# A recurrent attention layer and an FFN on one core: from 128-step chunks with per-head products to 64-step chunks with block-diagonal 128x128 products and the FFN woven in

## The chip, the cores and the metric

The kernel runs on one core of one Trainium2 chip. The time is that of the core from its first to its last instruction, in device microseconds (us). Each comparison is made on one chip, with runs of the kernel before among the others. The engines are PE (TensorE, with PEld for its weight loads), DVE (VectorE), ACT (ScalarE), POOL (GpSimd) and SP (SyncE), which only issues DMAs here.

## The reference, cut to what matters

```python
# 4 batches x 8 heads, 768 steps, head_dim 40; per head a 40x40 state
for t in range(S):
    y[:, :, t] = einsum('bhd,bhde->bhe', rt, state)
    Sa    = einsum('bhde,bhe->bhd', state, at)
    state = state * wt[:, :, None, :] - einsum('bhd,bhe->bhde', Sa, bt) \
            + einsum('bhd,bhe->bhde', vt, kt)
x = y.transpose(0, 2, 1, 3).reshape(3072, 320)       # tokens x (heads*40)
out = square(maximum(x @ w_in, 0)) @ w_out           # 320 -> 2048 -> 320
```

A kernel does not walk 768 steps. It takes a chunk of steps at once: products of k, b, a, r and v of the chunk, scaled by cumulative products of w, give the outputs within the chunk under a causal mask, and a 40x40 state per head is carried from chunk to chunk.

## The kernel before

Six chunks of 128 steps. Each chunk is prepared (cumulative decays by FP32 products, transposes of r, v, k, a), then worked in eight quads of four heads. A head has 40 channels, so an operand indexed by channel occupies 40 rows of the array, and one indexed by time 128. After the last chunk the FFN runs alone.

```python
# prep, once per chunk (FP32 products)
nc.tensor.matmul(out=cs[:, 0:n], lhsT=UTI[:], rhs=lnW[:, s0:s1], ...)      # FP32
nc.tensor.matmul(out=rep[:, 0:8*D], lhsT=SEL127[:], rhs=GAM[:, c0:c0+8*D], ...)
# stage2, once per quad: 40-row and 128-row weights alternate
for i in range(4):
    nc.tensor.matmul(out=mstp[:, i, :], lhsT=AT[pb:pb + D, prs[i], :],      # 40 rows
                     rhs=ST2[pb:pb + D, prs[i], :], start=True, stop=False)
    nc.tensor.matmul(out=mstp[:, i, :], lhsT=Em[:, i, :],                   # 128 rows
                     rhs=Vp[:, hhs[i], 0:D], start=False, stop=True)
...
for i in range(4):
    nc.tensor.matmul(out=xtp[:, i, :], lhsT=AT[pb:pb + D, prs[i], :],       # 40 rows
                     rhs=Zb[pb:pb + D, i, :], start=True, stop=False)
    nc.tensor.matmul(out=xtp[:, i, :], lhsT=Em[:, i, :],                    # 128 rows
                     rhs=CmT[:, i, :], start=False, stop=True)
... # yp, ytmp, YS, stp, state, and 32 small DMAs per chunk that gather YS into XT
# then the FFN, 512 tokens at a time
for g in range(3):
    nc.tensor.matmul(out=hp[:], lhsT=WIN[g][:, j*128:(j+1)*128],
                     rhs=XTg[g][:, tb*512:(tb+1)*512], start=(g==0), stop=(g==2))
nc.scalar.activation(out=hsb[:], in_=hp[:], func=ACTF.Copy)
nc.vector.scalar_tensor_tensor(out=Gt[:, j, :], in0=hsb[:], scalar=0.0, in1=hsb[:],
                               op0=ALU.max, op1=ALU.mult)
```

The scheduler of the framework decides the order of instructions on each engine, within the data dependences; the source order is a hint to it.

## Time and profile before

The median is 550.71 us (2 runs, 549.3 to 552.12).

| stretch | us | what stands out |
|---|---|---|
| start | about 45 | input DMA, first prep |
| six chunks | about 387 | PE busy 97%, clock 0.66 |
| FFN | about 118 | PE busy 97%, clock 0.98 |

The page, parts 1 and 2: the busy time of each engine, and tenths of 40 equal slices of the span.

```profile
PE 500.9 (91%) x3570; PEld 304.5 (55%) x3576; DVE 292.6 (53%) x478; ACT 230.4 (42%) x403; POOL 49.3 (9%) x54
...
PE   0609999999999999999999999999999799999997
...
PEclk9957566856559558595668755796555799999999
```

PE looks full from the start to the end, but the PEclk row (the granted clock) shows that through the chunks it was mostly granted half to two thirds of its clock, and steadily all of it only in the FFN (last eight slices). The view by windows says the same in numbers. Its columns are the window, its length, busy time and count for each engine, granted clock, DMA share and GB/s.

```profile
130.00:190.00 60.00, 58.10 (x465) 36.92 (x464) 35.65 (x62) 22.46 (x39) 4.65 (x5) 0.66 0.33 53
...
435.00:550.00 115.00, 111.39 (x652) 64.24 (x655) 59.92 (x92) 65.32 (x116) 0.00 (x0) 0.99 0.10 35
```

The timeline inside a quad. Columns: start, duration, engine, line, operation, output<-inputs, rows*columns of the weights, the moving tile, count.

```profile
153.33 0.31 PE L292 MATMUL yp_1357<-XmT,Btn 128*40 128x128 bf16 x1
...
153.44 0.31 PE L290 MATMUL yp_1357<-CmT,Kp 128*40 128x128 bf16 x1
...
154.03 0.28 PE L282 MATMUL xtp_1585<-Zb,AT 40*128 40x128 bf16 x1
...
154.25 0.29 PE L284 MATMUL xtp_1585<-CmT,Em 128*128 128x128 bf16 x1
...
154.47 0.29 PE L282 MATMUL xtp_1585<-Zb,AT 40*128 40x128 bf16 x1
```

Read the starts, not the durations, because matmuls are pipelined. The yp products, all with 128-row weights, start 0.105 us apart (the mean of six starts; the two shown differ by 0.11). The xtp products, whose weights alternate between 40 and 128 rows, start 0.22 us apart. Both move 128 columns, at the same clock (0.50 in that window).

### The profile page before, as it was taken

The page shows a single profiled execution, that of the slowest core. Times are in us where ns is not written, and L with a number is a line of the kernel's source. Part 1 is how long each engine was busy: PE and PEld are TensorE (multiplying, and loading weights), DVE is VectorE, ACT ScalarE, POOL GpSimd, SP SyncE. Part 2 cuts the span into 40 slices and gives each one's busy share as a digit, 9 for nine tenths or more (in the row PEclk, how much of TensorE's full clock was granted, in tenths as well). Part 3 has the DMA queues.
Part 4 walks back from the last instruction along what each step waited for, and adds up shares of the span by engine and source line. Part 5 has one row for each costly group of instructions (what it writes and reads, how often), then busy time and mean ns, then how long its engine had stood idle before and what let it go on. Part 6 is the DMA issues. An engine that isn't in the chain of part 4 may idle for free.

```text
span 550.1 us, 8764 instructions
## 1 busy us (share of the span) xinstructions
PE 500.9 (91%) x3570; PEld 304.5 (55%) x3576; DVE 292.6 (53%) x478; ACT 230.4 (42%) x403; POOL 49.3 (9%) x54
## 2 busy tenths in 40 slices
PE   0609999999999999999999999999999799999997
PEld 0207546655667545765557665576666365566554
DVE  0126448634566446755467553775655536634752
ACT  1705542644125532255324325352112446744762
POOL 9903000011000200002001010000000000000000
PEclk9957566856559558595668755796555799999999
DMA  9999335633327330934108291000000010011011
GB/s 159 189 186 180 53 54 80 76 53 51 53 49 109 54 51 8 146 56 82 27 7 117 39 128 26 6 6 8 7 7 10 4 49 17 33 48 37 19 42 50
DMA packets 163577, 32.69 MB, mean 59 GB/s; under 512 B 158096, under 2 KB 163216, under 8 KB 163536
## 3 DMA queue, kind: packets, MB, share of 16 engines
q1 hardware_dynamic: 161088, 29.50, 34.5%
q0 software_dynamic: 2448, 2.62, 2.8%
q8 instruction: 28, 0.46, 0.4%
q14 instruction: 13, 0.11, 0.1%
HBM read 28.84 MB, written 3.93 MB: 60 GB/s over the span
## 4 chain that ended last, share of the span: by engine, by line
PE 86%; DMA 5%; SPq 3%; ACT 2%; DVE 2%; issue 1%; ACTq 0%; DVEq 0%
PE hp L360 11%; PE trp L198 5%; PE cs L157 5%; PE rep L181 4%; DMA NB<-in_b_dram 4%; SPq L131 3%; PE trw L213 2%; ACT Zb L271 1%; ACT AT L204 1%; DVE Ap L175 1%; PE op_5950 L374 0%; PE op_5910 L374 0%; PE op_5717 L374 0%; PE op_5544 L374 0%; PE op_5371 L374 0%
## 5 line engine op out<-in xcount | busy, mean ns | idle before, releaser
L367 DVE SCALAR_TENSOR_TENSOR Gt<-hsb 128x512 bf16<-128x512 bf16 x96 | 62.5, 692 | 49.6 <-ACT hsb L366 49.6
L366 ACT ACTIVATE hsb<-hp 128x512 bf16<-128x512 f32 x96 | 57.1, 597 | 12.3 <-DMA XT_82<-YS 5.5
L157 PE MATMUL cs<-lnW,UTI 128*128 128x512 f32 (+1 forms) x36 | 30.9, 972 | 18.7 <-ACT lnW L148 18.7
L374 PEld LDWEIGHTS <-Gt 128*128 128x128 bf16 x384 | 37.6, 98 | 15.5
L181 PE MATMUL rep<-GAM,SEL_74 128*128 128x320 f32 x48 | 25.8, 666 | 14.6 <-DVE GL_166 L187 14.2
L360 PE MATMUL hp<-XT_80,WIN_93 128*128 128x512 bf16 x96 | 37.5, 391 | 0.5 <-issue 0.2
L360 PE MATMUL hp<-XT_78,WIN_90 128*128 128x512 bf16 x90 | 35.0, 389 | 3.0 <-ACT hsb L366 2.4
L360 PE MATMUL hp<-XT_82,WIN_96 128*128 128x512 bf16 x96 | 37.6, 392 | 0.0
L297 DVE TENSOR_TENSOR YS<-ytmp,GT 40x512 bf16<-40x512 f32 x48 | 32.7, 681 | 0.5
L274 PEld LDWEIGHTS <-AT 40*128 40x128 bf16 x192 | 19.0, 99 | 20.1 <-issue 13.1
L292 PEld LDWEIGHTS <-Btn 128*40 128x40 bf16 x192 | 24.0, 130 | 11.0 <-issue 9.2
L284 PEld LDWEIGHTS <-Em 128*128 128x128 bf16 x192 | 19.3, 101 | 19.4 <-issue 2.1
L282 PEld LDWEIGHTS <-AT 40*128 40x128 bf16 x192 | 18.7, 98 | 19.1 <-issue 4.7
L290 PEld LDWEIGHTS <-Kp 128*40 128x40 bf16 x192 | 23.6, 123 | 4.1 <-issue 2.2
L276 PEld LDWEIGHTS <-Em 128*128 128x128 bf16 x192 | 19.5, 101 | 10.1 <-issue 2.8
L145 ACT ACTIVATE Rp<-NR 128x1280 bf16<-128x1280 f32 x6 | 7.6, 1269 | 40.7 <-PE trp L198 30.6
L181 PEld LDWEIGHTS rep<-GAM,SEL_74 128*128 128x128 f32 x48 | 11.5, 273 | 19.6 <-issue 17.0
L172 DVE TENSOR_TENSOR Kp<-NK,GAMI 128x1280 bf16<-128x1280 f32 x6 | 8.9, 1488 | 24.3 <-ACT GAMI L160 24.3
L157 PEld LDWEIGHTS cs<-lnW,UTI 128*128 128x128 f32 x36 | 9.1, 306 | 22.8 <-issue 20.8
L143 POOL MEMSET Rp<- 128x768 bf16 x6 | 4.5, 745 | 179.4 <-PE trp L198 179.4
L304 PEld LDWEIGHTS <-Vp 128*40 128x40 bf16 x192 | 15.1, 110 | 9.4 <-issue 7.3
L267 PEld LDWEIGHTS <-S_84 40*40 40x40 bf16 x192 | 14.9, 115 | 9.4 <-issue 6.0
(1138 smaller groups left out, 1074.1 us busy)
## 6 DMA issues: line engine op xcount, KB each, us to landing
NR<-in_r_dram SPq DMA_DIRECT2D x6, 640.0 KB
NK<-in_k_dram SPq DMA_DIRECT2D x6, 640.0 KB
NV<-in_v_dram SPq DMA_DIRECT2D x6, 640.0 KB
NW<-in_w_dram SPq DMA_DIRECT2D x6, 640.0 KB
NA<-in_a_dram SPq DMA_DIRECT2D x6, 640.0 KB
NB<-in_b_dram SPq DMA_DIRECT2D x6, 640.0 KB
out_dram<-osb SPq DMA_DIRECT2D x24, 160.0 KB
WOUT<-in_moe_w_out_dram POOLq DMA_DIRECT2D x1, 1280.0 KB, 14.5
```

The lines of the kernel that those rows point to most:

```text
L157: nc.tensor.matmul(out=cs[:, 0:n], lhsT=UTI[:], rhs=lnW[:, s0:s1], start=True, stop=True)
L181: nc.tensor.matmul(out=rep[:, 0:8 * D], lhsT=SEL127[:], rhs=GAM[:, c0:c0 + 8 * D], start=True, stop=True)
L198: nc.tensor.transpose(out=trp[:, j * L:(j + 1) * L], in_=srcv, identity=IDb[:])
L276: nc.tensor.matmul(out=mstp[:, i, :], lhsT=Em[:, i, :], rhs=Vp[:, hhs[i], 0:D], start=False, stop=True)
L284: nc.tensor.matmul(out=xtp[:, i, :], lhsT=Em[:, i, :], rhs=CmT[:, i, :], start=False, stop=True)
L290: nc.tensor.matmul(out=yp[pb:pb + D, i, :], lhsT=Kp[:, hhs[i], 0:D], rhs=CmT[:, i, :], start=(i == 0), stop=False)
L292: nc.tensor.matmul(out=yp[pb:pb + D, i, :], lhsT=Btn[:, hhs[i], 0:D], rhs=XmT[:, i, :], start=False, stop=(i == 3))
L297: nc.vector.tensor_tensor(out=YS[pb:pb + D, pc:pc + 4, :], in0=ytmp[pb:pb + D, :, :], in1=GT[pb:pb + D, pc:pc + 4, 0:L], op=ALU.mult,)
L360: nc.tensor.matmul(out=hp[:], lhsT=WIN[g][:, j * 128:(j + 1) * 128], rhs=XTg[g][:, tb * 512:(tb + 1) * 512], start=(g == 0), stop=(g == 2),)
L366: nc.scalar.activation(out=hsb[:], in_=hp[:], func=ACTF.Copy)
L367: nc.vector.scalar_tensor_tensor(out=Gt[:, j, :], in0=hsb[:], scalar=0.0, in1=hsb[:], op0=ALU.max, op1=ALU.mult,)
L374: nc.tensor.matmul(out=op_[:], lhsT=Gt[:, j, s_ * 128:(s_ + 1) * 128], rhs=WOUT[:, j, :], start=(j == 0), stop=(j == 15),)
```

## The change

The intent: the array is always used as one 128x128 square, PE's waits are filled with FFN products, and PE's idle time shrinks. Two heads from different batches are paired. k and b of one chunk of 64 steps are stacked along the partitions, and so are a and r; a and r are then transposed into block-diagonal form (ARB), so that one 128x128 product serves both heads. A second step corrects the solve of the triangular system. The FFN of chunk c-1 (input products) and c-2 (output products) is emitted inside the units of chunk c. There are 12 chunks of 4 units of 4 pairs, that is 48 units. The FP32 products of the preparation become two bf16 products each, of a high and a low part (lhi, llo).

The names in the diff and in the traces: ef is the product of kt (k and b, transposed) with the a half of ARB, and em is ef under the causal mask; mp, mb, mc are the steps of the solve; tv and vt are its transposed result; cx is vt's product with r, and cm is cx under the mask; sp is the state, yp the output of attention; hp, hs, g and op belong to the FFN; GI and GP are the cumulative decays, and gr, GLI, GLT the decay row that ends the chunk. The diff, cut to its core (the old body is removed whole):

```diff
-    L = 128
+    L = 64
+    NU = 4
+    def load_rv(c):                       # r and v: POOL's DMA queue, cast to bf16 on the way
+            nc.gpsimd.dma_start(out=AR[c % 2][64:128, :, s, 0:D], in_=r[...])
+            nc.gpsimd.dma_start(out=VM[c % 2][p0:p0 + 64, :, s, 0:D], in_=v[...])
+    # zero fills AR, VM, KB, STB, SB on DVE; ARB on POOL; then masks UTI, UTE, MSK on POOL
...
+    def prep_k(c):
+            nc.vector.tensor_tensor(out=kb[o, :, s, 0:D], in0=n["K"][q], in1=gi[q], op=ALU.mult)
+        gr = drp.tile([2, NPAIR, D], FP32, ...)                  # DRAM
+        nc.sync.dma_start(out=gr[:], in_=gi[63:128:64])          # the decay row
+                nc.sync.dma_start(out=gli[64*s:64*s+D, :], in_=gr[s].rearrange("x e -> e x"))
+        nc.vector.reciprocal(out=glt[:], in_=gli[:])
...
+    def prep_tr(c, u):
+        nc.scalar.activation(out=kt[:], in_=tk[:], func=ACTF.Copy)
+        nc.vector.tensor_copy(out=arb[0:64, 4*u:4*u+4, 0:4:2, :], in_=ta[0:64]...)
+        nc.vector.tensor_copy(out=arb[64:128, 4*u:4*u+4, 1:4:2, :], in_=ta[64:128]...)
+    def st_ef(c, u):  ... em = ef * MSK                          # DVE
+    def st_m0(c, u):  ... mb = -mp, two halves                   # ACT
+    def st_cor(c, u): ... vm = mb - mc, two halves               # DVE
+    def st_tvm(c, u): ... vt = copy(tv)                          # DVE
+    def st_cx(c, u):
+        nc.scalar.activation(out=cm[:], in_=cx[:]..., func=ACTF.Copy)
+        for s in range(2):
+            nc.gpsimd.affine_select(out=cm[q], in_=cm[q], pattern=[[0, 8], [1, 64]], ...)
+    def st_st(c, u):  ... STB = sp * GLT, two halves             # DVE
+    def st_y(c, u):   ... ys = yp * gp, two halves               # DVE
+    def st_ts(c, u):  ... SB = copy(tp), two halves              # DVE
+    def ff_in(c, jj):
+        nc.scalar.activation(out=hs[:], in_=hp[:], func=ACTF.Relu)
+        nc.vector.tensor_tensor(out=G[c][:, 2*jj:2*jj+2, :], in0=hs[:], in1=hs[:], op=ALU.mult)
...
+    prep_head(0)
+    for u in range(3):
+        prep_tr(0, u)
+    N[1] = load(1)
+    load_rv(1)
+    load_weights()
...
+    for n, (c, u) in enumerate(units):
+        st_tvm(c, u); ff_in(c - 1, 2*u); st_cx(c, u); st_ef(*nx); ff_out(c - 2, 2*u)
+        ... prep of chunk c+1 ...; st_m0(*nx); ff_in(c - 1, 2*u + 1); st_st(c, u)
+        st_y(c, u); st_cor(*nx); ff_out(c - 2, 2*u + 1); st_ts(c, u); prep_tr(*units[n + 3])
```

## The prediction

> **What bounds it now.** The profile page gives PE 500.9 us busy of 550.1 (91%), DVE 292.6, ACT 230.4. Windows of the trace split the span: about 45 us until the first chunk is prepared (the chain of waits there is input DMA), six chunks of 57 to 65 us in which PE is busy 97% but at a granted clock of only 0.66 to 0.71, and an FFN of 118 us at 0.98 that streams without gaps. So attention is 387 us, held by PE's instruction stream, not by arithmetic. In the timeline, at clock 0.50, products that alternate 40-row and 128-row weights (xtp) take 220 ns each, unmixed ones of the same width (yp) 105 ns; unmixed 128x128 transposes at clock 1.00 take 56 ns. The Trainium skill (TensorEngine Tiling, Key Properties) says that changing tiling mode drains TensorE; the mixed products agree.
>
> **The change.** Full 128x128 weights everywhere, FP32 products as bf16 high plus low, FFN woven in. From the instruction order: 48 units (12 chunks x 4), each about 72 products and 11,800 streamed columns: 4.9 us at clock 1.00, about 6.2 at 0.8. PE's work thus falls to about 240 to 300 us, and FFN products fill its waits.
>
> **What it adds is DVE work.** Per unit, with durations of before (512 columns from PSUM fp32 673 ns; 160 columns 317 ns; bf16 PSUM copy of 1024 692 ns, so 512 about 0.42 us; fp32 product of 1280 1488 ns, so 640 about 0.82): em 0.67, vt 0.42, correction 0.64, state 0.64, y 0.64, block-diagonal copies 0.84, state transpose 0.48, squares 2 x 0.42, xt 0.18, prep 6.4/4 = 1.6. Sum 6.9 us, 333 us in all (estimate), perhaps 15 less where neighbours overlap. The 0.42 of the squares assumes that two bf16 SBUF operands run at double rate, as the skill says (VectorE: DVE Perf Modes, perf-mode tier table); no instruction of before shows it. The half-partition pairs (64 x 160) pay the roughly 150 ns fixed part twice. ACT about 4.4 us per unit (211 us, with 11 pairs of table loads of 1.28), POOL about 3 (two selects of about 0.63, memsets, DMA issue).
>
> **Sum.** DVE becomes the busiest engine. Start about 20 us (half-size chunk, w first), tail about 10 us of FFN output products. Between, DVE's 320 us at 85 to 90% use: the unit's chain mc-vm-tv-vt-cx and ef-em-mp-mb-mc crosses PE, DVE and ACT, PE executes in order, three PSUM buffers serve ten tiles per unit, and the scheduler bunches FFN input products into one half of each chunk and output products into the other. That gives about 370 us. Total 400 us, range 355 to 445. Chances: faster 0.96, same 0.02, slower 0.02.
>
> **What would show it right.** DVE busy 310 to 340 us; a steady pitch of 7 to 8.5 us per unit, 28 to 34 per chunk; clock 0.75 to 0.95; 128-column products at 56 to 107 ns; squares near 420 ns; first unit at about 20 us; tail of at most 15 us.
>
> **What would make it wrong.** DVE squares or copies at single rate (plus 25 us or more); PE stalled for DVE, ACT or PSUM buffers so that the clock stays near 0.6 and PE becomes the limit again (430 or more); POOL's DMA issue and selects late for cx or v; slow small DMAs (the decay row through DRAM, scattered bf16 r and v) holding a chunk; or DVE instructions overlapping more than before (350 or less).

## The result, and the profile after

The changed kernel takes 448.28 us (2 runs, 446.34 to 450.22), and the ratio to the kernel before is 0.8131, with a 95% interval of 0.8028 to 0.8235. Repeated on another chip (run a0 below) it is 448.39 us and 0.8167 (0.8120 to 0.8215). A ratio here is the mean time of one kernel's runs over that of the other's runs of the same rounds, so it is not quite the ratio of the medians quoted. The direction was right, but 448 lies above the forecast's 400 and just outside its range of 355 to 445: the gain was 102 us where 151 was forecast.

The page after, parts 1, 2 and 4 (the last is the chain of waits, followed back from the end):

```profile
PE 315.3 (71%) x3480; PEld 221.3 (50%) x3480; DVE 350.7 (79%) x820; ACT 205.0 (46%) x394; POOL 149.7 (34%) x257
...
PE   0231767877877877877876886876877778777975
...
DVE  7442787997997997996997997997987987977841
...
PEclk9999998989999999998999989999999998999989
...
issue 41%; POOL 25%; PE 17%; DVE 16%; POOLq 0%; ACT 0%; DVEq 0%
```

PE's busy time fell by 186 us and its clock is now nearly full. DVE is the busiest engine. Two things stand out: in slices 2 to 4 (about 11 to 44 us) little runs: 4, 4 and 2 tenths on DVE, 2, 3 and 1 on PE, and the last two slices are thin. The windows view of the changed kernel, with the same columns as before:

```profile
20.00:40.00 20.00, 3.57 (x29) 2.81 (x28) 7.35 (x14) 2.23 (x5) 0.00 (x0) 1.00 1.12 171
...
140.00:180.00 40.00, 30.54 (x362) 21.75 (x363) 34.65 (x83) 22.07 (x42) 14.31 (x25) 1.00 0.54 55
...
420.00:445.00 25.00, 16.72 (x138) 11.43 (x135) 7.68 (x23) 6.68 (x12) 2.00 (x6) 0.90 0.11 28
```

From 20 to 40 us PE is busy for 3.57 of 20 us, DVE for 7.35 and POOL not at all, while the DMA engines move 171 GB/s. In the middle DVE is busy 34.65 of 40 us.

In the timeline, the 48 copies of vt mark the units. The first starts at 44.5 us, the last at 422.2, and between them the distance repeats every four units (8.06, 10.7, 7.2, 6.6 us), 32.6 us per chunk. The span of 444.3 us of the profiled run is therefore 44.5 + 377.7 + 22.1. The forecast had 20 + 370 + 10. **The middle was nearly right. The start and the tail were not.** The cut is not quite the forecast's: the first vt copy comes 4 us after em, DVE's first instruction of unit 0 proper, so this middle holds 47 of the 48 units. Counted by whole units, the middle is 386 us (48 x 8.04), and start and tail together are 59 us, where the forecast had 30.

The start in the timeline of the changed kernel (brackets: idle time of the engine before the instruction, and what ended it):

```profile
14.73 8.83 SPq L59 DMA_DIRECT2D NK<-in_k_dram  x2
...
17.75 0.45 PE L157 MATMUL cs<-lhi,UTI 128*128 128x320 bf16 x1 [17.75 <-POOL UTI L112]
...
18.44 1.21 POOL L132 DMA_DIRECT2D WOUT<-in_moe_w_out_dram  x1
...
23.60 4.22 SPq L59 DMA_DIRECT2D NB<-in_b_dram  x1
...
27.94 4.19 SPq L169 DMA_DIRECT2D gr<-GI  x1
...
36.48 0.85 SPq L172 DMA_DIRECT2D GLI<-gr  x2
...
39.21 0.25 DVE L174 RECIPROCAL GLT<-GLI 128x16 f32<-128x16 f32 x1 [12.12 <-DMA GLI<-gr]
...
40.39 0.69 DVE L223 TENSOR_TENSOR em<-ef,MSK 128x512 bf16<-128x512 f32 x1
```

First, PE's first product waits 17.75 us for the mask UTI, because the scheduler placed the masks on POOL behind zero fills and eleven DMA issues. Second, the decay row (gr, then GLI) was ready to leave at 19.5 us, when GI was done, but SP was still issuing chunk 1's loads, and issues that take 0.8 us each elsewhere take 4 us here. Third, the reciprocal of the decay row stands in front of em in DVE's list of instructions, so DVE, and with it everything, waits 12.12 us for two transfers of 2.5 KB. (In run e4 below the reciprocal stands later, and em runs at 25.0 us, before it.)

The tail, in PE's and ACT's lines of the timeline:

```profile
427.44 7.18 PE L339 MATMUL hp<-xt,WIN 128*128 128x256 bf16 x48 [0.45 <-DVE xt L329]
...
434.46 2.34 PE L352 MATMUL op<-WOUT,g 128*128 128x320 bf16 x16
...
437.32 2.33 PE L352 MATMUL op<-WOUT,g 128*128 128x320 bf16 x16 [0.53 <-ACT osb L357]
...
439.69 0.44 ACT L357 ACTIVATE osb<-op 128x320 f32<-128x320 f32 x1 [2.42 <-PE op L352]
```

After the last vt copy, 5.2 us finish the unit, 7.0 us are the last chunk's FFN input products, 5.2 us its output products, and 4.6 us pass from osb to the end, with the last store. The forecast had counted the output products alone.

### The profile page after: what moved, and what is told of

Same layout as the page of the kernel before. It is cut to its first block, busy times and chain, and to the rows that moved or that the text cites. A ratio compares the mean times of both kernels' runs of the same rounds, so it can differ in the third digit from the quotient of the medians.

```text
span 444.3 us, 9156 instructions
## 1 busy us (share of the span) xinstructions
PE 315.3 (71%) x3480; PEld 221.3 (50%) x3480; DVE 350.7 (79%) x820; ACT 205.0 (46%) x394; POOL 149.7 (34%) x257
## 4 chain that ended last, share of the span: by engine, by line
issue 41%; POOL 25%; PE 17%; DVE 16%; POOLq 0%; ACT 0%; DVEq 0%
POOL cm L270 15%; PE hp L339 6%; POOL AR L68 4%; DVE VM L249 3%; DVE em L223 2%; PE op L352 2%; DVE ys L306 2%; PE yp L297 2%; DVE ARB L204 2%; POOL ARB L82 2%; DVE ARB L201 2%; DVE SB L315 1%; POOL VM L289 1%; POOL VM L288 1%; PE cx L265 1%
## 5 line engine op out<-in xcount | busy, mean ns | idle before, releaser
L270 POOL TENSOR_SCALAR_AFFINE_SELECT cm<-cm 64x512 bf16<-64x512 bf16 x96 | 77.2, 804 | 243.0 <-ACT cm L267 198.1
L343 ACT ACTIVATE hs<-hp 128x512 bf16<-128x512 f32 x96 | 57.2, 596 | 73.7 <-DVE g L344 39.9
L339 PE MATMUL hp<-xt,WIN 128*128 128x256 bf16 x576 | 87.0, 277 | 1.4 <-DVE xt L329 1.3
L352 PE MATMUL op<-WOUT,g 128*128 128x320 bf16 x384 | 70.6, 305 | 5.6 <-DVE g L344 4.7
L339 PEld LDWEIGHTS <-WIN 128*128 128x128 bf16 x576 | 54.6, 100 | 11.2 <-issue 2.4
L223 DVE TENSOR_TENSOR em<-ef,MSK 128x512 bf16<-128x512 f32 x48 | 32.6, 678 | 22.9 <-PE ef L221 22.6
L196 ACT ACTIVATE kt<-tk 128x512 bf16<-128x512 bf16 x48 | 28.6, 596 | 45.7 <-PE tk L194 45.7
L237 ACT ACTIVATE VMB<-mp 64x160 bf16<-64x160 f32 x96 | 28.6, 298 | 36.1 <-PE mp L233 34.8
L344 DVE TENSOR_TENSOR g<-hs 128x512 bf16<-128x512 bf16 x96 | 39.2, 426 | 6.8 <-ACT hs L343 5.4
L352 PEld LDWEIGHTS <-g 128*128 128x128 bf16 x384 | 33.0, 99 | 20.1 <-DVE g L344 11.5
L297 PE MATMUL yp<-KB,cm 128*128 128x80 bf16 x192 | 21.3, 209 | 28.9 <-POOL cm L270 28.8
L285 DVE TENSOR_TENSOR STB<-sp,GLT 64x160 bf16<-64x160 f32 x96 | 30.7, 320 | 13.4 <-PE sp L282 12.5
L306 DVE TENSOR_TENSOR ys<-yp,GP 64x160 bf16<-64x160 f32 x96 | 30.9, 322 | 4.9 <-PE yp L297 3.2
L194 PE MATMUL tk<-IDb,KB 128*128 128x128 bf16 x192 | 20.7, 236 | 10.3 <-DVE ys L306 6.8
L68 POOL DMA_DIRECT2D AR<-in_r_dram x24 | 19.7, 827 | 22.6 <-PE hp L339 20.1
```

Source lines behind the costliest of these rows:

```text
L68: nc.gpsimd.dma_start(out=AR[c % 2][64:128, :, s, 0:D], in_=r[2 * s:2 * s + 2, :, sl, :].rearrange("b h t e -> t (b h) e"))
L223: nc.vector.tensor_tensor(out=em[:], in0=ef[:], in1=MSK[:].rearrange("p (x y) t -> p x (y t)", y=2), op=ALU.mult)
L270: nc.gpsimd.affine_select(out=cm[q], in_=cm[q], pattern=[[0, 8], [1, 64]], compare_op=ALU.is_gt, fill=0.0, base=0, channel_multiplier=-1)
L285: nc.vector.tensor_tensor(out=STB[q, us, s, 0:D], in0=sp[q, :, s, :], in1=GLT[c % 2][q, us].unsqueeze(2).broadcast_to((64, 4, D)), op=ALU. ...
L297: nc.tensor.matmul(out=yp[:, i], lhsT=cm[:, 2 * i:2 * i + 2, :].rearrange("p y t -> p (y t)"), rhs=kb[:, pr, :, 0:D], start=False, stop=(i ...
L306: nc.vector.tensor_tensor(out=y[q, h0:h0 + 4, :], in0=yp[q, :, s, :], in1=gp[q, 4 * u:4 * u + 4, :], op=ALU.mult)
```

## The experiments

Each has three rounds beside the kernel before. Two groups of edits are to the changed kernel; one is to the kernel before. The unedited baseline is a0.

| run | edit | us | ratio to before (95%) |
|---|---|---|---|
| a0 | none | 448.39 | 0.8167 (0.8120 to 0.8215) |
| e2 | masks first | 443.82 | 0.8077 (0.8027 to 0.8127) |
| e3 | decay row ahead of chunk 1's loads | 441.08 | 0.8028 (0.7980 to 0.8076) |
| e4 | e2 + e3 + late reciprocal | 440.68 | 0.8019 (0.7964 to 0.8074) |
| e5 | weights late | 436.80 | 0.7959 (0.7891 to 0.8027) |
| e6 | e4 + e5 | 432.29 | 0.7870 (0.7802 to 0.7939) |
| e7 | upper block-diagonal copy to ACT | 429.39 | 0.7808 (0.7755 to 0.7862) |
| e8 | mask of cx on DVE | 459.38 | 0.8356 (0.8301 to 0.8411) |
| e9 | mask of cx in one POOL product | 454.14 | 0.8273 (0.8219 to 0.8327) |
| e10 | e6 + e7 | 415.73 | 0.7557 (0.7524 to 0.7590) |
| e11 | e10 + half of the squares to ACT | 409.37 | 0.7445 (0.7411 to 0.7478) |
| b1 | kernel before, products grouped | 474.94 | 0.8641 (0.8594 to 0.8687) |

All gave correct results. Differences against a0 below are differences of ratios times 550 us, since the calls ran on different chips. Each ratio is known to about 0.6%, so such a difference is known to about 4 us. The lines shown are of the profile that was read at the time; a profile of the same kernel taken again differs from it, by up to about 1.5 us in the places quoted.

### a0: the baseline

> The changed kernel once more, unedited, so that the edits below have a baseline on the same chip. Both theories: about 447 us, 0.81 of the kernel before; first vt copy at about 44.5 us, last at about 422, pitch 8.04 us per unit.

It came out at 448.39 us, with the first vt copy at 45.3 us, the last at 425.9, and a mean distance of 8.10 us.

### e2: the masks first

```diff
     N = {0: load(0)}
+    ones_b = ...; IDb = ...; UTI, UTE, MSK = ...     # moved up, ahead of the zero fills and load_rv(0)
```

> Only the triangle masks and the identity are built before the zero fills and the POOL queue's DMA issues. The first cumulative product cs waited 17.8 us for the mask UTI; it should start at about 13 us. Theory A (the start is a chain, and its longest link is the decay row's DMA, queued behind the next chunk's loads; DVE stands 12.1 us at the reciprocal that waits for it): almost nothing, 0 to -3 us, because the decay row still waits. Theory B (the masks on POOL are the longest link): -4 to -5 us. Theory C (the start is bound by input traffic of about 170 GB/s whatever the order): 0.

The gain was about 5 us, as theory B had it, though within its 4 us it does not exclude theory A's 0 to 3. The first product now starts at 14.1 us and the first vt copy at 39.9. But DVE still waits 8.0 us for the decay row, so B is a link, not the longest one.

### e3: the decay row first

```diff
-                nc.sync.dma_start(
+                DEC[c] = nc.sync.dma_start(
                     out=gli[64 * s:64 * s + D, :], ...)
-    N[1] = load(1)
+    with tc.issue_after(DEC[0].ins):          # order of issue only
+        N[1] = load(1)
```

> Only the order on the SP queue is changed: the loads of chunk 1 are issued behind the first decay row's three DMAs. Theory A: the decay row lands near 26 us in place of 39, the reciprocal's wait falls from 12.1 us to about 1 to 3, and the run gains 9 to 12 us. Theory B: 0. Theory C: at most -3 us, and the wait moves to the loads of chunk 1.

The gain was 7.6 us, less than the 9 to 12 of theory A: the reciprocal ran at 31.9 us, not at 26. The decay row left at 19.5 us and its scatter at 24.4, and 7.5 us passed until it had landed.

### e4: all start edits

```diff
-        nc.vector.reciprocal(out=glt[:], in_=gli[:])                       # in prep_k
+        if u == 0:                                                         # in st_st
+            nc.vector.reciprocal(out=GLT[c % 2][:], in_=GLI[c % 2][:])
```

(with the edits of e2 and e3)

> Masks first, decay row first, and the reciprocal emitted just before its first use. Theory A: the links add once the longest is gone, first vt copy at 27 to 31 us in place of 44.5, the run gains 13 to 18 us, and the pitch of the units stays 8.0 us. Theory C: at most -4 us.

The gain was 8 us, not 13 to 18; theory A as stated failed. The first vt copy is at 38.7. The timeline shows why:

```profile
18.99 1.27 SPq L173 DMA_DIRECT2D GLI<-gr  x2
...
32.89 0.25 DVE L278 RECIPROCAL GLT<-GLI 128x16 f32<-128x16 f32 x1 [7.20 <-DMA GLI<-gr]
```

The scatter (two transfers of 2.5 KB) left SP at 19 us with nothing of SP's in front of it, and still took nearly 14 us. What was in flight with it were chunk 1's loads, which SP issued right behind it, and the FFN weights, issued by POOL at 16.9 to 19.7 us (5.2 MB read in FP32). So a new theory was formed: the weights crowd out the start's transfers.

### e5: the weights late

```diff
-    load_weights()                                     # after load_rv(1)
+        if n == 0:
+            with tc.issue_after(POOLED[(0, 0)].ins):   # unit 0's last zero fill on POOL
+                load_weights()
```

> One edit to the changed kernel: the four FFN weight loads are issued on POOL's queue behind unit 0's last zero fill, near 30 us, in place of 14 to 19 us; they are needed from about 70 us. Theory A2 (formed from the start runs: the weights' transfers crowd out the decay row and chunk 1's loads, which is why the decay row's scatter of 2.5 KB still took 12 us when issued at 19 us): chunk 1's loads and the decay row land 8 us or more earlier, the reciprocal's wait of 12.1 us falls below 5, the run gains 7 to 12 us. Rival C2 (the decay row's trip through DRAM with 4-byte elements is slow by itself): gain below 3 us.

The gain was 11.4 us by this edit alone, the largest of the single start edits, and the first vt copy moved to 31.5 us. The timeline of this run:

```profile
18.73 0.60 SPq L169 DMA_DIRECT2D gr<-GI  x1
...
20.82 0.84 SPq L172 DMA_DIRECT2D GLI<-gr  x2
...
27.52 0.25 DVE L174 RECIPROCAL GLT<-GLI 128x16 f32<-128x16 f32 x1
...
36.41 0.61 POOL L129 DMA_DIRECT2D WIN<-in_moe_w_in_dram  x1
```

The reciprocal no longer waits. Part of the gain is not the transfers': without the weights' issues in front of them the masks were ready earlier too, and the first product started at 16.1 us in place of 17.75. The KB products behind it moved by 0.8 us. The same scatter, with chunk 1's loads still around it but no weights, landed in at most 6.7 us. Rival C2 (slow by itself) fails. The Trainium skill (DMA: Bandwidth & Descriptors, Queues, rings and completion order) says that an SDMA engine takes its queues in turn at packet granularity, so a small transfer on one queue can share an engine with a large one on another; the runs agree with this in effect (nearly 14 us against 6.7), but none separates the turn-taking from sheer traffic.

### e6: the start edits and the weights together

> Masks first, decay row ahead of chunk 1's loads, late reciprocal, and the weights late. Theory A2: decay row landed by about 23 us, first vt copy at 28 to 31 us in place of 44.5, total 14 to 17 us below the unedited kernel (about 432). Rival C2: no better than the start edits without the weights' move (about -8 us).

The gain was 16.3 us, within 14 to 17. The first vt copy is at 29.7 us. Of the 24.5 us by which the start had been underestimated, 15 to 16 are thus recovered by order alone. From then on the distances of the units are as before (10.3, 7.2, 6.6, 8.1).

### e7: less work on DVE

```diff
-        nc.vector.tensor_copy(
+        nc.scalar.activation(
             out=arb[64:128, 4 * u:4 * u + 4, 1:4:2, :],
-            in_=ta[64:128]...)
+            in_=ta[64:128]..., func=ACTF.Copy)
```

> The upper half of the block-diagonal copy (428 ns, once per unit) goes from DVE to ACT; nothing else. Theory D (the steady part is bound by DVE, which is idle only about 3.4 us of each 32.6 us chunk): the pitch falls by 0.35 to 0.43 us per unit and the run by 15 to 20 us. Rival P (it is bound by the chain through POOL's selects, for which PE waits 28.8 us in all, and DVE's busy share is a symptom): 0 to -3 us.

The gain was 19.7 us, the upper end of theory D. A copy of 0.43 us taken from DVE 48 times moved the whole kernel by nearly its own sum (20.5 us). The part 1 lines of the pages, first of a0 and then of e7:

```profile
PE 318.3 (71%) x3480; PEld 224.1 (50%) x3480; DVE 350.4 (78%) x820; ACT 205.0 (46%) x394; POOL 150.0 (33%) x257
...
PE 311.2 (73%) x3480; PEld 219.0 (51%) x3480; DVE 317.9 (74%) x772; ACT 231.0 (54%) x442; POOL 147.0 (34%) x257
```

DVE's busy time fell by more, 32.5 us, partly because its SBUF products happened to meet POOL less often (KB<-NB,GI has a mean of 816 ns here and about 1120 in a0). So the match with 20.5 us is partly luck: the run gained 0.6 of what DVE was relieved of.

### e8: more work on DVE, none on POOL

```diff
-        nc.scalar.activation(out=cm[:], in_=cx[:]..., func=ACTF.Copy)
-        for s in range(2):
-            nc.gpsimd.affine_select(out=cm[q], in_=cm[q], ...)
+        nc.vector.tensor_tensor(out=cm[:], in0=cx[:]..., in1=MSK[:], op=ALU.mult)
```

> The causal mask of cx is applied by DVE out of PSUM (one product of 512 columns, 0.67 us), in place of a copy on ACT and two selects on POOL; POOL's and ACT's links leave the chain, DVE gains 32 us of work. Theory D: slower by 15 to 32 us[...]. Rival P: faster by 10 us or more.

It was slower by 10.4 us, below the expected 15 to 32 but on theory D's side. Rival P needed a gain. The chain lost two links that the profile had named, and the kernel became slower. The granted clock was lower too (0.908 to 0.936, in a0 0.976 to 0.981), but that is unlikely to explain it: of e5's runs the two at 0.933 took 435.3 and 435.9 us and the two at 0.976 took 437.7 and 439.1. The size follows DVE's busy time, which rose by 11.3 us and not by 33:

```profile
PE 334.0 (73%) x3480; PEld 236.4 (52%) x3480; DVE 361.7 (79%) x868; ACT 180.5 (39%) x346; POOL 72.4 (16%) x161
```

The lines of one product of prep show where most of the rest went, first in a0 and then in e8 (min/median/max ns, first and last start):

```profile
L180 DVE TENSOR_TENSOR KB<-NB,GI x24: 816/1180/1259, 21.3 to 385.3; 64x640 bf16<-64x640 f32 x24
```

```profile
L180 DVE TENSOR_TENSOR KB<-NB,GI x24: 752/820/823, 21.4 to 395.6; 64x640 bf16<-64x640 f32 x24
```

With POOL's selects gone, the same product takes 820 ns in place of 1180. It is slowed only where it meets POOL: its twin KB<-NK,GI, of the same shape, has a median of 822 ns in a0 (its slowest took 1178). The Trainium skill (GPSIMD Engine Reference, Specifications) says that POOL's SBUF interfaces are shared with VectorE and contended by instructions with two SBUF inputs; the trace agrees, a slowdown of 44% in the median here. The forecast's 0.82 us for this product was right only without POOL.

### e9: one POOL product in place of two selects

```diff
-        for s in range(2):
-            nc.gpsimd.affine_select(out=cm[q], in_=cm[q], ...)
+        nc.gpsimd.tensor_tensor(out=cm[:], in0=cm[:], in1=MSK[:], op=ALU.mult)
```

> The changed kernel with one 128-partition product with the mask on POOL in place of two 64-partition selects; DVE's list of work is unchanged. Theory D: within 6 us of the unedited kernel, and what moves is DVE's busy time (POOL now reads two operands, so DVE's SBUF products may be slowed more or less). Rival P: 20 us or more faster, since PE waited 28.8 us for the selects.

It was 5.8 us slower, within theory D's 6 us. It shortens POOL's link (one product of 1.19 us for two selects of 0.80 each in the unedited kernel's profile) and gained nothing; DVE's busy time rose to 359.2 us. It is weak evidence against P on its own, since the link shrank only by a few tenths of a us, but e7 gained without touching the selects, e8 lost without them, and no run here speaks for P.

### e10: start and offload together

> The start edits with the weights late, and the upper block-diagonal copies on ACT, together. If the start (-16 us) and the DVE-bound middle (-19 us) are separate stretches, the gains add: 411 to 416 us.

It came out at 415.73 us, 33.5 us below a0 by ratio, where the single gains sum to 36.0. The two stretches are nearly separate.

### e11: half of the squares to ACT

```diff
+        if jj % 2:
+            nc.scalar.activation(out=G[c][...], in_=hs[:], func=ACTF.Square)
+        else:
             nc.vector.tensor_tensor(out=G[c][...], in0=hs[:], in1=hs[:], op=ALU.mult)
```

> The same, and every second square of the FFN on ACT: DVE loses 48 x 0.426 = 20 us, ACT gains 48 x 0.6 = 29 us. Theory D: another 12 to 20 us, 393 to 402 us. If DVE is no longer the limit after the first offload, and the chain over PE, ACT and POOL is: 405 us or more.

It came out at 409.37 us: a gain of 6.2 us, where theory D had 12 to 20. This is a miss for a DVE-only view. The windows view from 100 to 300 us, of a0, e7 and e11 in turn:

```profile
100.00:300.00 200.00, 153.58 (x1778) 107.76 (x1778) 174.26 (x410) 106.53 (x203) 71.63 (x124) 0.98 0.54 63
...
100.00:300.00 200.00, 159.34 (x1867) 111.23 (x1865) 162.23 (x403) 124.47 (x235) 71.95 (x130) 1.00 0.56 65
...
100.00:300.00 200.00, 160.06 (x1911) 113.69 (x1907) 162.91 (x391) 144.20 (x276) 74.44 (x131) 1.00 0.60 70
```

DVE was busy 87% of the middle in a0. It was down to 81% with e7's edit alone and is at 81% here, with PE at 80% and ACT at 72%, so no single engine stands out as the limit any more. In e7, e8, e9 and this run (against e10) the time followed DVE's busy time, but by 0.6, 0.9, 0.7 and here 0.4 of its change: the further DVE is relieved, the less it is worth. What the remaining waits between the engines are worth was not tested. This version beats both kernels, by 141 us and about 40 us.

### b1: the kernel before, with its products grouped

```diff
         for i in range(4):
             nc.tensor.matmul(out=mstp[:, i, :], lhsT=AT[pb:pb + D, prs[i], :],
-                             rhs=ST2[pb:pb + D, prs[i], :], start=True, stop=False)
+                             rhs=ST2[pb:pb + D, prs[i], :], start=(i == 0), stop=False)
+        for i in range(4):
             nc.tensor.matmul(out=mstp[:, i, :], lhsT=Em[:, i, :],
-                             rhs=Vp[:, hhs[i], 0:D], start=False, stop=True)
+                             rhs=Vp[:, hhs[i], 0:D], start=False, stop=(i == 3))
         # the same for xtp
```

> An edit to the kernel before, not to the changed one: in xtp and mstp the four products with 40-row weights are issued together, then the four with 128-row weights, in place of alternating; the same products. In PE's order the changes between 40-row and 128-row weights fall from about 940 to 390. Theory M (the kernel before lost its time to these changes): each costs about 0.1 us (220 against 105 ns in the trace), so 550 fewer take 30 to 60 us off. Rival K (the low clock of about 0.67 is what costs, and the order of the products does not matter): under 10 us.

The kernel before falls to 474.94 us, a gain of 76 us, more than theory M's 30 to 60 and far from rival K's 10. The page and a stretch of the timeline of this run:

```profile
PE 414.8 (88%) x3576; PEld 262.5 (56%) x3576; DVE 290.9 (62%) x478; ACT 228.8 (48%) x403; POOL 49.4 (10%) x54
...
PEclk9985997999595786955778558965568999999999
```

```profile
204.22 0.60 PE L283 MATMUL xtp<-Zb,AT 40*128 40x128 bf16 x4
204.76 0.61 PE L286 MATMUL xtp<-CmT,Em 128*128 128x128 bf16 x4
205.30 0.61 PE L245 MATMUL ee<-AT,KT 40*128 40x128 bf16 x4
```

At the same clock of 0.50, four products take 0.54 us, 135 ns each, where the alternating ones took 220. If a product costs 105 ns, a group pays 0.11 to 0.12 us once, and the alternating order paid it at every product. At clock 1.00 (55.6 to 56.4 us in the trace of the kernel before) the alternating xtp products start 0.16 us apart and unmixed ones 0.056, so there too a change costs about 0.10 us. In the order of the two traces' weight loads the changes between 40-row and 128-row weights fall from 1008 to 424 (the expectation had counted about 940 and 390), so 584 fewer: about 60 us at 0.10 to 0.11 each. The other 15 us or so are not accounted for one by one. The mean granted clock rose from 0.744 to 0.818, and whether that is an effect of the shorter gaps or a cause of part of the gain was not told apart.

Two rivals fail by the trace of the kernel before, at the same clock of 0.50. One is that 40-row weights are slow by themselves, or that the flags which b1 changes as well (start and stop on every product) cost the time. The cc products have 40 rows throughout and carry both flags, and four of them take 0.56 us until the next product, with one change included:

```profile
149.77 0.63 PE L251 MATMUL cc_1560<-RT,VT 40*128 40x128 bf16 x4
150.33 0.29 PE L290 MATMUL yp_1357<-CmT,Kp 128*40 128x128 bf16 x1
```

The other is that two products in a row into the same slice of PSUM wait for each other: the yp products do just that, at 0.105 us. The rows are not the whole rule, though: where only the columns of the weights change (40x40 in zp, then 40x128), the next product also starts 0.24 us later (median of 23 pairs) and not 0.107.

The meaning for the change is large: 76 of the 102 us that the rewrite gained can be had in the old layout by regrouping sixteen products per quad. That does not prove that the rewrite's gain consists of the same 76 us, because it has other limits; it shows that full 128x128 operands were not the only way to remove the mixing.

## Why the prediction was right or wrong

**What bounds the kernel before: right.** Mixing of 40-row and 128-row weights on PE was named from the timeline, with 220 against 105 ns, and b1 shows that the order of the products is the cause. The prediction gave it no size; the expectation of b1 did, 30 to 60 us, and 76 were measured. The Trainium skill (TensorEngine Tiling, Key Properties), which says that a change of tiling mode drains TensorE, agrees with the trace; that products of 40 and of 128 rows run in different tiling modes is inferred, since no view shows the mode.

**PE's work after: right in direction.** Four 128-column products start about 55 ns apart in the changed kernel, as two groups in its timeline show by their starts 0.22 us apart:

```profile
208.38 0.39 PE L265 MATMUL cx<-ARB,vt 128*128 128x128 bf16 x4
208.60 0.39 PE L221 MATMUL ef<-ARB,kt 128*128 128x128 bf16 x4
```

The clock, forecast at 0.75 to 0.95, was 0.976. PE's busy time of 315 us is just above the 240 to 300 forecast. What each part of the rewrite gave was not tested: besides the mixing, FP32 products went, of which cs and rep alone had kept PE busy for 30.9 and 25.8 us.

**DVE becomes the limit: right.** e7 and e8 show it in both directions. DVE's busy time was 350.7 us against 310 to 340. Of the 31 us above the 320 that the sum went on with, about 9 us are zero fills at the start, which the sum left out, and about 17 us are prep products and casts slowed by POOL (7.9 us per chunk measured by the group means, 6.4 forecast, and 6.4 in e8, without the selects). Squares were forecast at 420 ns on the double rate that the Trainium skill states (VectorE: DVE Perf Modes, perf-mode tier table) and measured 426; the halves of 160 columns at 317 and measured 319 to 322.

**The middle: right.** 377.7 us against "about 370 us"; 8.04 us per unit, inside 7 to 8.5, and 32.6 us per chunk, inside 28 to 34. The reasoning holds as well as the number: between the first and the last vt copy DVE was busy for 324 us, 86%, where the forecast had 320 us at 85 to 90%.

**The step that failed: "Start about 20 us (half-size chunk, w first), tail about 10 us".** The start took 44.5 us to the first unit. The order on SP and POOL had been read, but only for what each instruction does, not for what waits behind it. The forecast's reason, a chunk of half the size with w loaded first, speaks of chunk 0's loads alone; what held DVE was the wait of 12.12 us for the decay row, issued behind chunk 1's loads and in flight beside the FFN weights. The list "what would make it wrong" did name "slow small DMAs (the decay row through DRAM ...) holding a chunk", but the sum had no term for it. e5 and e6 put 11 and 16 us of the excess down to the order of transfers and issues. The remaining 10 us of start (29.7 us in e6) were not tested one by one. The tail was 22.1 us: the forecast term held the output products and left out the last unit's end, the input products of the last chunk and the final store. Start and tail together were 36.6 us too small, of the 44.3 us by which the profiled run exceeds 400; the middle makes the other 7.7. By whole units it is 28.6 and 15.7 us. By either count the start is the largest term, and with its order mended (e6) the kernel takes 432 us.

**A warning from the profile's own chain.** The chain of waits after the change names POOL with 25% and the selects as its costliest line, and PE waited 28.8 us for them. e8 took them away and the kernel became slower. A chain names what released a step last; it does not say what the step would have waited for next. The line of that wait in part 5 of the page:

```profile
L297 PE MATMUL yp<-KB,cm 128*128 128x80 bf16 x192 | 21.3, 209 | 28.9 <-POOL cm L270 28.8
```

## What to carry to other kernels

Before a rewrite that makes all operands full, try grouping the products by the shape of their weights: here sixteen moved products per quad in the old kernel gave 76 us. When a scheduler orders the queues, walk the first chunk by hand along every engine's and queue's list, and ask of each early instruction what stands in front of it; bulk loads that are needed late belong behind the first small transfer that everything waits for. And where one engine is far busier than the others in the steady part (here DVE with 87%), try moving its work before touching the waits that the chain names.

## What the Trainium skill lacked or had wrong

- TensorEngine Tiling (Array Packing), Key Properties: it says that a change of tiling mode drains TensorE but gives no cost. Here it is 0.10 to 0.12 us per change, at clock 0.50 and at 1.00, and 584 changes fewer came with a gain of 76 us.
- GPSIMD Engine Reference, Specifications: it names the contention with VectorE but no size, and the skill's page on SBUF, which treats it further, has no figure for this pair of instructions. Here a DVE product of two SBUF tensors (64x640) has a median of 1180 ns with POOL's selects in the kernel and 820 ns without.
- DMA: Bandwidth & Descriptors: no figure for a small transfer beside a bulk one on another queue. Here a scatter in two transfers of 2.5 KB needed nearly 14 us beside chunk 1's loads and 5.2 MB of weight reads (e4), and at most 6.7 us without the weights (e5).
- ScalarE: Activation LUTs, What ACT_TABLE_LOAD costs: it gives about 1283 ns plus about 1380 ns of drain for each switch. The 1283 ns agree. The drain is not visible here: a load at 42.52 us is followed by the activation at 43.82, 1.30 us later.
- TensorE: Matmul & The Clock Gate, PE-mode transpose: it gives about 275 ns for a 128x128 bf16 transpose in a kernel. Here the duration of a tv transpose (its end is modelled by the profile) has a median of 219 ns, and in the kernel before, at clock 1.00, eight weight loads and transposes follow each other within 0.45 us of weight loading, about 56 ns each.
